# Loading an attention output projection's weights in two whole-tile transfers, split by rows instead of columns

## The chip, the cores and the metric

The kernel runs on one core of one Trainium2 chip. The metric is the device time of one execution in microseconds. Five engines of the core matter here: TensorE (matmuls), VectorE, ScalarE, GpSimd (POOL) and SyncE (SP), which here only issues DMAs. DMAs issued by SP and by POOL are carried out by the core's 16 DMA engines. Before the change, three runs gave 818.97, 821.54 and 822.07 us, a median of 821.54 us.

## The reference

The input `x` is 2048 rows of 1024 (bfloat16). It is normalised by rows (layer norm without weights). From the result `xn` two branches are computed and joined:

- branch A: `qkv = xn @ wqkv` (1024 by 3072), 32 heads of 32 columns each. Each position attends to 8 positions: itself and those 2, 4, ... 14 before it. The softmax-weighted sum of `v` is multiplied by `wo` (1024 by 1024).
- branch B: `h = silu(xn @ w1) * (xn @ w3)` (each 1024 by 3584), then `h @ w2` (3584 by 1024).

```
s = _A_ref(xn, A_wqkv, A_wo)          # ends in  o.reshape(B, S, D) @ wo
g = silu(_B_ref(xn, B_w1, B_w3, B_w2))
return x + s * g
```

## The kernel before

The 2048 rows are done in four chunks `c` of 512 (`CH`). For a chunk, TensorE does in this order:

1. `qkv` (L273): 24 products of 8 matmuls with `xnT`, the normalised, transposed rows. Chunk 0 has these between its first blocks of `w1` and `w3`.
2. `up_block` (L258) for 14 blocks `fb`: two column groups of `w1` and two of `w3`, each product 8 matmuls. ScalarE applies silu, VectorE multiplies, and this gives the 28 `ht` tiles.
3. `down_half` (L447) for the first half `dh = 0` of the output columns: 7 blocks `fb` of 16 matmuls, with four accumulators.
4. `down_half` for `dh = 1`; after its third block (sixth in chunk 0), `wo_proj` (L416) is put in: 8 products of 8 matmuls. In the last chunk `wo_proj` comes between the halves, and the second half runs row tile by row tile (`last_half`, L483).

The attention itself runs beside these on VectorE, in pieces handed out by `Side` according to estimated costs. Its data cross partitions by DMAs from POOL: 16 transfers `L<-E` before the softmax (L333) and 16 transfers `Pr<-pb` after it (L374). The products with `v` (L385) and their sums (L396) then give `oT`, the left operand of `wo_proj`.

All code is scheduled by hand: each engine takes its instructions in the order in which they were written. On SP's queue that order is, late in a chunk: the last `w1` and `w3` tiles (L167, from six buffers, asked for three blocks ahead), the output weights (`load_wo`, called after block `fb == 10`, L198), then for each block of `down_half` one `w2` tile (`load_w2`, L185), with a transposing DMA of the next chunk's rows (L676) beside it in the first four blocks. The `w2` tiles have three buffers: the first three of a chunk are loaded long before; the tile for the fourth block is issued when the matmuls of the first are done. In the last chunk there is nothing to transpose. POOL loads the residual `xres` (L472, 1 MB) once per chunk.

`oT` has on partition `r*32 + h` the element `r*8 + j` of head `h`, for `j` from 0 to 7. So the weights must lie the same way: row `h*32 + r*8 + j` of `wo` belongs on partition `r*32 + h`. In DRAM, 8 consecutive rows of `wo` (`j`) form one contiguous run of 16 KB. `load_wo` takes two blocks of 128 partitions by 4096 elements from a pool of nine that the attention's tiles also use. Block `dh` holds all eight `j` and 512 of the 1024 columns, loaded by four DMAs of 32 partitions, with 8 runs of 1 KB for each partition. `wo_proj` uses block `dh` alone for the four products of a column half.

Of the kernel before, what the change touches and what calls it, by code (L numbers as in the profile page):

```python
# [45 lines left out]
def kernel(  # L46
# [11 lines left out]
    nc = tc.nc  # L58
    P = 128
    S, D, F = 2048, 1024, 3584  # L60
    Dh, W, DIL = 32, 8, 2
    KT = D // P
    CH = 512
# [5 lines left out]
    NJ = 8  # L69
    NR = 4  # L70
# [9 lines left out]
    w1_r = B_w1.rearrange("(kt p) f -> p kt f", p=P)  # L80
    w3_r = B_w3.rearrange("(kt p) f -> p kt f", p=P)
    w2_r = B_w2.rearrange("(ft p) n -> p ft n", p=P)
    wo_r = A_wo.rearrange("(h r j) n -> r h j n", r=NR, j=NJ)
    wqkv_r = A_wqkv.rearrange("(kt kp) c -> kp kt c", kp=P)

    const = ctx.enter_context(tc.tile_pool(name="const", bufs=1))
# [19 lines left out]
    def block(name):  # L106
        return blk.tile([P, 4096], BF16, tag="blk", name=name)
# [6 lines left out]
    for st in range(2, NST):  # L114
# [10 lines left out]
        out=ident[:], in_=ident[:], compare_op=ALU.not_equal, fill=1.0,  # L125
# [5 lines left out]
        out=maskb[:], in_=maskb[:], compare_op=ALU.is_ge, fill=-1.0e9,  # L131
# [60 lines left out]

    def load_wo():
        was = []
        for dh in range(2):
            wa = block("wo").rearrange("p (j n) -> p j n", n=CH)
            for r in range(NR):
                nc.sync.dma_start(out=wa[r * 32:(r + 1) * 32, :, :], in_=wo_r[r, :, :, dh * 512:(dh + 1) * 512])  # L198
            was.append(wa)
        return was  # L200


# [205 lines left out]
    def wo_proj(c, was):  # L408
        side.flush()
        oT = att["oT"]  # L410
        s_sb = block("s_sb").rearrange("p (st d) -> p st d", st=NST)
        for dh in range(2):
            for st in range(NST):
                ps = psum_aux.tile([P, CH], FP32, tag="aux", name="ps_wo")
                for j in range(NJ):
                    nc.tensor.matmul(  # L416
                        ps[:], lhsT=oT[:, j, st * P:(st + 1) * P], rhs=was[dh][:, j, :],
                        start=(j == 0), stop=(j == NJ - 1),
                    )
                nc.scalar.copy(out=s_sb[:, st, dh * 512:(dh + 1) * 512], in_=ps[:])  # L420
                side.step(GRP)
        return s_sb
# [131 lines left out]
    def bring0(st):  # L554
# [16 lines left out]
        out=junk[:], in_=x0[2][:], func=ACTF.Square, bias=nm[:], scale=1.0 / 32.0, accum_out=mv0[2][:, 1:2],  # L571
# [54 lines left out]
    for fb in range(1, LEAD):  # L626
        w1t, w3t = take_w(("1", fb)), take_w(("3", fb))
        for i in range(2):
            pss = []
            for wt in (w1t, w3t):  # L630
                ps = psum_mm.tile([P, CH], FP32, tag="mm", name=f"gu0_{fb}_{len(pss)}")
# [7 lines left out]
    for t in range(3):  # L639
        for j in range(NJ):  # L640
            ps = psum_mm.tile([P, CH], FP32, tag="mm", name="ps_qkv")
# [6 lines left out]
        for half in range(2):  # L648
            nc.sync.dma_start(
                out=wperm[half * 4:(half + 1) * 4, :, t * NJ:(t + 1) * NJ, :].rearrange("kt kp j p -> kp kt (j p)"),  # L650
                in_=pmh[t, half].rearrange("kp kt j p -> kp kt (j p)"),
# [5 lines left out]
    for c in range(NCH):  # L657
        if c > 0:
            qkv(c, xnT)
        was = None  # L660
        for fb in range(LEAD if c == 0 else 0, FB):
            blk_hts = up_block(c, xnT, fb)
            hts = hts + blk_hts if hts is not None else blk_hts
            if fb == 10:
                was = load_wo()
# [14 lines left out]
        if c + 1 < NCH:  # L680
            state = {}

            def mid(fb, c=c):
                if fb == (WO_AT if c else WO_AT0) - 1:
                    state["s"] = wo_proj(c, was)
                    for st in range(NST):
                        side.add(1.38, lambda st=st: finish(c, st, 0, 512, gts[st], state["s"], xres, nc.gpsimd))

            gts1 = down_half(c, 1, hts, mid)
            side.flush()  # L690
            s_sb = state["s"]
            for st in range(NST):
                side.add(1.38, lambda st=st, c=c, gts1=gts1, s_sb=s_sb, xres=xres: finish(
                    c, st, 512, 512, gts1[st], s_sb, xres, nc.gpsimd))
            xnT = xnT_next
            hts = None
        else:
            s_sb = wo_proj(c, was)
            for st in range(NST):
                finish(c, st, 0, 512, gts[st], s_sb, xres, nc.gpsimd)  # L700
            last_half(c, hts, s_sb, xres)
# [30 lines left out]
```

## Time and profile before

| | before |
|---|---|
| median of three runs | 821.54 us |
| profiled execution | 819.93 us |
| its span, first to last instruction | 818.2 us |
| TensorE matmul busy | 808.8 us (99%), 3817 matmuls |
| VectorE, ScalarE, POOL busy | 481.4, 206.1, 95.3 us |
| mean granted TensorE clock | 0.999 |
| DMA: data, mean rate | 152.69 MB, 187 GB/s |
| `wo` loads | 32 issues of 256 KB, median 9.2 us from issue to landing |
| `w1`, `w3`, `w2` loads | 168 issues of 512 KB, median 4.6 us from issue to landing |
| `wo_proj` matmuls (L416) | 256, in the chain with 13.81 us per chunk |

A line of the page's groups gives the line of the code, the engine and operation, the tiles written and read with their sizes, the count, and then busy time and mean duration. Matmul durations overlap, since matmuls are pipelined. "SPq" is an instruction that SP's queue handles without SP being busy, DMA issues among them. In the list of waits, the last three numbers are the total in us, how many times, and the longest. In the chain in order of time, they are the start, the length in us, and the work with its count. In a timeline, the first two numbers are start and length of a merged group of instructions. In a table of windows, the columns are the window, its length, busy time of TensorE, its weight loads, VectorE, ScalarE and POOL with counts, the clock, the DMA share and the rate in GB/s. The DMA share is the busy time of packets over 16 engines; packets that overlap can bring it above 1.

### The profile page before, as it was taken

The page shows a single profiled execution, that of the slowest core. Times are in us where ns is not written, and L with a number is a line of the kernel's source. Part 1 is how long each engine was busy: PE and PEld are TensorE (multiplying, and loading weights), DVE is VectorE, ACT ScalarE, POOL GpSimd, SP SyncE. Part 2 cuts the span into 40 slices and gives each one's busy share as a digit, 9 for nine tenths or more (in the row PEclk, how much of TensorE's full clock was granted, in tenths as well). Part 3 has the DMA queues.
Part 4 walks back from the last instruction along what each step waited for, and adds up shares of the span by engine and source line. Part 5 has one row for each costly group of instructions (what it writes and reads, how often), then busy time and mean ns, then how long its engine had stood idle before and what let it go on. Part 6 is the DMA issues. An engine that isn't in the chain of part 4 may idle for free.

```text
span 818.2 us, 9549 instructions
## 1 busy us (share of the span) xinstructions
PE 808.8 (99%) x3817; PEld 372.5 (46%) x3817; DVE 481.4 (59%) x489; ACT 206.1 (25%) x319; POOL 95.3 (12%) x176
## 2 busy tenths in 40 slices
PE   8999999999999999999999999999999999999997
PEld 5444444444444444444444444444444444444444
DVE  6619947693229765692224968489111695759432
ACT  6552133011432132101133213310223321311120
POOL 0000041301100223000110030400000004130010
PEclk9999999999999999999999999999999999999999
DMA  9992698795454786879255588869925548696810
GB/s 289 347 371 74 195 211 194 167 307 180 130 149 140 219 193 182 180 197 307 87 180 153 144 221 181 196 134 230 295 92 180 152 133 203 167 210 144 255 51 26
DMA packets 221085, 152.69 MB, mean 187 GB/s; under 512 B 19568, under 2 KB 209136, under 8 KB 221040
## 3 DMA queue, kind: packets, MB, share of 16 engines
q1 hardware_dynamic: 214224, 135.55, 60.8%
q0 software_dynamic: 6528, 16.26, 8.1%
q8 instruction: 30, 0.49, 0.2%
q10 hardware_dynamic: 288, 0.26, 0.1%
q14 instruction: 15, 0.12, 0.1%
HBM read 130.02 MB, written 10.49 MB: 172 GB/s over the span
## 4 chain that ended last, share of the span: by engine, by line
PE 97%; DMA 2%; ACT 0%; DVE 0%; SPq 0%; issue 0%
PE gu L258 45%; PE ps_qkv L273 20%; PE acc L447 19%; PE ps_wo L416 7%; PE acc L483 3%; DMA wt<-in_B_w_dram 2%; PE gu L273 2%; PE gu L584 1%; DMA x<-in_A_x_dram 0%; PE tp L543 0%; ACT xnT L547 0%; ACT junk L560 0%; SPq L112 0%; DVE x L207 0%; DVE gt L433 0%
## 5 line engine op out<-in xcount | busy, mean ns | idle before, releaser
L258 PE MATMUL gu<-xnT_next,wt 128*128 128x512 bf16 x1344 | 290.6, 379 | 0.0
L258 PEld LDWEIGHTS <-wt 128*128 128x128 bf16 x1696 | 166.0, 98 | 200.1
L447 PE MATMUL acc<-wt,ht 128*128 128x512 bf16 x784 | 170.7, 379 | 1.3 <-DMA wt<-in_B_w_dram 1.3
L247 DVE TENSOR_TENSOR ht<-sg,gu 128x512 bf16<-128x512 bf16 x112 | 75.8, 680 | 92.1 <-PE gu L258 67.6
L245 ACT ACTIVATE sg<-gu 128x512 bf16<-128x512 f32 x112 | 65.9, 597 | 247.7 <-PE gu L258 232.8
L273 PE MATMUL ps_qkv<-xnT_next,wt 128*128 128x512 bf16 x576 | 124.8, 379 | 0.0
L303 DVE TENSOR_TENSOR prod<-qT,kT 128x4096 bf16<-128x4096 bf16 x32 | 73.1, 2285 | 86.4 <-ACT kT L277 86.3
L447 PEld LDWEIGHTS <-ht 128*128 128x128 bf16 x784 | 76.7, 98 | 94.1 <-issue 1.8
L273 PEld LDWEIGHTS <-wt 128*128 128x128 bf16 x640 | 62.6, 98 | 75.3
L433 DVE TENSOR_TENSOR gt<-gt,s_sb 128x512 f32<-128x512 f32 (+1 forms) x33 | 22.2, 674 | 122.0 <-ACT gt L427 63.3
L258 PE MATMUL gu<-xnT,wt 128*128 128x512 bf16 x352 | 76.1, 379 | 0.0
L333 POOL DMA_DIRECT2D L<-E x64 | 37.1, 587 | 295.0 <-DVE E L318 190.1
L385 DVE TENSOR_TENSOR pv<-Pr,vT 128x4096 bf16<-128x4096 bf16 x28 | 63.2, 2283 | 0.0
L314 DVE TENSOR_TENSOR prod<-prod 128x2048 bf16<-128x2048 bf16 x64 | 61.1, 955 | 1.4
L416 PE MATMUL ps_wo<-wo,oT 128*128 128x512 bf16 x256 | 55.9, 379 | 0.0
L427 ACT ACTIVATE gt<-acc 128x512 f32<-128x512 f32 (+1 forms) x33 | 19.3, 584 | 141.1 <-PE acc L447 119.6
L374 POOL DMA_DIRECT2D Pr<-pb x64 | 36.8, 583 | 107.6 <-DVE pb L367 101.9
L273 PE MATMUL ps_qkv<-xnT,pm 128*128 128x512 bf16 x192 | 41.6, 379 | 0.0
L435 POOL DMA_DIRECT2D out_dram<-o_t x28 | 15.3, 545 | 209.4 <-DVE o_t L434 204.9
L416 PEld LDWEIGHTS <-oT 128*128 128x128 bf16 x256 | 25.0, 98 | 30.2
L420 ACT CAST s_sb<-ps_wo 128x512 bf16<-128x512 f32 x32 | 18.7, 585 | 77.9 <-PE ps_wo L416 77.9
L396 DVE TENSOR_TENSOR oT<-oT,pv 128x4096 bf16<-128x4096 bf16 x16 | 36.6, 2288 | 0.3
(67 smaller groups left out, 371.4 us busy)
## 6 DMA issues: line engine op xcount, KB each, us to landing
wt<-in_B_w_dram SPq DMA_DIRECT2D x168, 512.0 KB, 4.6
wt<-wperm SPq DMA_DIRECT2D x36, 512.0 KB, 5.4
wo<-in_A_wo_dram SPq DMA_DIRECT2D x32, 256.0 KB, 9.2
raw<-in_A_wqkv_dram SPq DMA_DIRECT2D x6, 1024.0 KB, 10.2
wperm<-pm SPq DMA_DIRECT2D x6, 1024.0 KB, 9.4
L<-E POOLq DMA_DIRECT2D x64, 64.0 KB, 5.8
Pr<-pb POOLq DMA_DIRECT2D x64, 64.0 KB, 4.2
xres<-in_A_x_dram POOLq DMA_DIRECT2D x4, 1024.0 KB, 6.9
```

The lines of the kernel that those rows point to most:

```text
L245: nc.scalar.activation(out=sg[:], in_=g_ps[:], func=ACTF.Silu)
L247: nc.vector.tensor_mul(ht[:], sg[:], u_ps[:])
L258: nc.tensor.matmul(ps[:], lhsT=wt[:, kt, i * P:(i + 1) * P], rhs=xnT[:, kt, :], start=(kt == 0), stop=(kt == KT - 1),)
L273: nc.tensor.matmul(ps[:], lhsT=lhs(kt), rhs=xnT[:, kt, :], start=(kt == 0), stop=(kt == KT - 1))
L303: nc.vector.tensor_mul(prod, qT[:], kT[:, :, o:o + CH])
L314: nc.vector.tensor_add(prod[:, 0:n, :], prod[:, 0:n, :], prod[:, n:2 * n, :])
L333: nc.gpsimd.dma_start(out=L4[sq * 32:(sq + 1) * 32, r, :, :], in_=E[r * 32:(r + 1) * 32, :, sq * P:(sq + 1) * P],)
L374: nc.gpsimd.dma_start(out=Pr[r * 32:(r + 1) * 32, :, sq * P:(sq + 1) * P], in_=pb[sq * 32:(sq + 1) * 32, :, :],)
L385: nc.vector.tensor_mul(dst, Pr[:, w, :].unsqueeze(1).to_broadcast([P, NJ, CH]), vT[:, :, o:o + CH])
L396: nc.vector.tensor_add(a, a, b)
L416: nc.tensor.matmul(ps[:], lhsT=oT[:, j, st * P:(st + 1) * P], rhs=was[dh][:, j, :], start=(j == 0), stop=(j == NJ - 1),)
L447: nc.tensor.matmul(accs[st][:], lhsT=hts[f][:, st * P:(st + 1) * P], rhs=w2t[:, i, :], start=(f == 0), stop=(f == FT - 1),)
```

## The change

The view of `wo` in DRAM now has `j` and the columns as one contiguous dimension of 8192 elements. A block holds half of that dimension: four of the eight `j`, with all 1024 columns. It is loaded by one DMA of 1 MB with one run of 8 KB for each of the 128 partitions. In `wo_proj`, each product of 8 matmuls takes its first four from one block and its last four from the other. The issue's place in SP's queue, the blocks' sizes and the matmuls' sizes stay as they are.

```
-    wo_r = A_wo.rearrange("(h r j) n -> r h j n", r=NR, j=NJ)
+    wo_r = A_wo.rearrange("(h r j) n -> r h (j n)", r=NR, j=NJ)
...
     def load_wo():
         was = []
-        for dh in range(2):
-            wa = block("wo").rearrange("p (j n) -> p j n", n=CH)
-            for r in range(NR):
-                nc.sync.dma_start(out=wa[r * 32:(r + 1) * 32, :, :], in_=wo_r[r, :, :, dh * 512:(dh + 1) * 512])
-            was.append(wa)
+        for half in range(2):
+            wa = block("wo")
+            nc.sync.dma_start(out=wa[:], in_=wo_r[:, :, half * 4096:(half + 1) * 4096])
+            was.append(wa.rearrange("p (j n) -> p j n", n=D))
         return was
...
                 for j in range(NJ):
                     nc.tensor.matmul(
-                        ps[:], lhsT=oT[:, j, st * P:(st + 1) * P], rhs=was[dh][:, j, :],
+                        ps[:], lhsT=oT[:, j, st * P:(st + 1) * P], rhs=was[j // 4][:, j % 4, dh * 512:(dh + 1) * 512],
                         start=(j == 0), stop=(j == NJ - 1),
                     )
```

## The prediction

> **What bounds the kernel now.** I read four views in this order: the page's busy rows and chain, the table of waits, the windows around the output-weight loads, and SyncE's timeline with the landings of its DMAs.
>
> The page and the chain come first.
>
> ```profile
> PE 808.8 (99%) x3817; PEld 372.5 (46%) x3817; DVE 481.4 (59%) x489; ACT 206.1 (25%) x319; POOL 95.3 (12%) x176
> PEclk9999999999999999999999999999999999999999
> PE 97%; DMA 2%; ACT 0%; DVE 0%; SPq 0%; issue 0%
> ```
>
> TensorE is the bound: busy for 808.8 of 818.2 us at the full granted clock, and 97% of the chain. The waits say how much a better-timed transfer could give back:
>
> ```profile
> PE acc L447 <- DMA wt<-in_B_w_dram: 1.3, 2, 1.0
> ```
>
> TensorE waits 1.3 us in the whole run for weights, always for the down projection's (L447), never for `wo`. So the change can gain hardly more than 1.3 us, and its reach downward is set by what it does to transfers that TensorE does need. The chain, in order of time, gives the deadlines:
>
> ```profile
> 149.33 10.37 PE acc L447 x48
> ...
> 350.05 34.53 PE acc L447 x160
> ...
> 550.35 6.92 PE acc L447 x32
> ...
> 751.78 24.17 PE acc L447 x112
> ```
>
> The down projection of the four chunks starts at 149.33, 350.05, 550.35 and 751.78 us. Its `w2` tiles have three buffers, filled long before; the fourth tile is asked for when the first has been used. Three tiles take 10.37 us of matmuls (the first of these lines), so that fourth tile must have landed by 159.7, 360.4, 560.7 and 762.1 us.
>
> SyncE's timeline, in chunk 0, has the `wo` loads and what comes next on the queue:
>
> ```profile
> 129.06 6.41 SPq L198 DMA_DIRECT2D wo<-in_A_wo_dram  x8
> 152.81 0.39 SPq L185 DMA_DIRECT2D wt<-in_B_w_dram  x1
> 153.29 1.34 SPq L676 DMA_TRANSPOSE xnT_next<-x_t  x1
> ```
>
> The other chunks issue `wo` from 329.78, 530.08 and 731.82. Between `wo` and that fourth `w2` tile, SyncE issues nothing for 17 us.
>
> Then the windows (us; busy times of five engines; clock; DMA share; GB/s), one with nothing but `wo` on the DMA engines and one of large 128-partition loads at the start:
>
> ```profile
> 137.00:139.50 2.50, 2.50 (x14) 1.12 (x12) 2.43 (x4) 0.60 (x1) 0.00 (x0) 1.00 1.13 219
> 40.00:50.00 10.00, 10.00 (x48) 4.55 (x47) 2.01 (x2) 6.62 (x9) 0.00 (x0) 1.00 1.09 374
> ```
>
> Both keep the 16 DMA engines full (shares of 1.13 and 1.09), yet `wo`, which goes to 32 partitions at a time, gets 219 GB/s, or 13.7 per engine, where the other gets 374, or 23.4 per engine. The landings of the `wo` transfers, and of the weights of the last stage (755 to 776):
>
> ```profile
> DMA to landing us min/median/max: 7.0/9.2/11.1
> DMA to landing us min/median/max: 3.4/3.7/4.8
> ```
>
> **The change, part by part.**
>
> *Fewer issues.* 32 `wo` issues at a median of 478 ns become 8: some 11.5 us less on SyncE's queue. Zero for the end: SyncE is otherwise idle for those 17 us. The last of each chunk's eight issues also waits for an earlier weight tile (135.16 in chunk 0); that goes too, with nothing queued behind it. If that cover were gone, 6 us per chunk would stand ahead of the `w2` issue; it is not.
>
> *Matmuls.* 256 of them (L416), still 128x512 from contiguous runs of 512 columns: no change at 379 ns each. Every product now needs both tiles, and both are held to the end of `wo_proj`, 7 us longer for the first (half of the 13.81 us of L416). Their blocks come up again nine allocations later, in the next chunk's attention, over 40 us on: zero. The later landing of the pair costs nothing while it stays ahead of 194.65, 384.59, 586.02 and 775.96, when `wo_proj` starts.
>
> *The transfer itself.* Same 2.1 MB per chunk, in runs of 8 KB instead of 1 KB. What decides is over how many DMA engines it is spread. Every transfer in this trace has an outermost count of 32 or 128, a multiple of 16. The new source is (r, h, columns) with an outermost count of 4, and it can't be merged: h steps over 32 rows, r over 8. No row shows such a transfer. The bounds are 16 engines, if it is dealt out by the tile's 128 rows, and 4 engines, if by the source's outermost dimension. I take 4, because 4 units can't be dealt out evenly to more, and because the nearest rows (`wo` before, 32 units) leave no remainder that would show another way.
>
> The Trainium skill ("DMA: Bandwidth & Descriptors", section on why a DMA increments its semaphore by 16) has a rule for this which speaks against the change: a transfer uses the largest number of engines up to 16 that divides the slowest counts of both sides, here 4 and 128, hence 4. No row here shows it for a count under 16.
>
> *With 4 engines*, each carries 524 KB per chunk. At 23.4 GB/s that takes 22.4 us, at 13.7 it takes 38.3 us. I take 38.3: the low rate is `wo`'s own row, for writes into one group of 32 partitions, and the four shares walk through four such groups in step, on 4 partitions at a time, which is narrower still. The Trainium skill ("SBUF — State Buffer", "Door 1: The DMA port swizzle") says that partitions p and p+32 share a port, which would pair the shares two by two; the 219 against 374 GB/s agrees with such sharing.
>
> Start of the stream: the old first transfer landed 7.0 us after its issue, 1.2 us of which was its own 256 KB at 219 GB/s; with some 1 us for completion (an estimate: half of the 2.0 us that the fastest 512 KB landing, 3.4 us, has over 1.4 us at 374 GB/s), it began 4.8 us after the issue, behind the weight tiles queued before it. End: 129.06 + 4.8 + 38.3 = 172.2, and 372.9, 573.2, 774.9.
>
> *What stands behind it.* The fourth `w2` tile has its share on all engines, those four too, behind `wo` on the same queue. After `wo` ends it takes 1.4 us of data and 1 us of completion. Landing 174.6 against a need at 159.7: TensorE waits 14.9 us in chunk 0. Chunk 1: 375.3 - 360.4 = 14.9; chunk 2: 575.6 - 560.7 = 14.9; chunk 3: 777.3 - 762.1 = 15.2. Sum 59.9 us.
>
> *POOL's transfers on the same engines.* `xres` (1 MB, four times) and, in chunk 0, the 16 `Pr` transfers (1 MB, issued 139.8 to 150.0) put 65.5 KB each on those engines while they are busy: five times 2.8 us at 23.4 GB/s if it all adds up, five times 4.8 at 13.7, nothing if they fill gaps that the paired engines leave. Bounds 0 and 24 us; I take 7, half of the middle, since an engine that serves POOL leaves its partner alone for that time. Late `Pr` would delay the `oT` products on VectorE, which end at 185.6 against 194.65 in chunk 0: 9 us of cover, and more once TensorE itself is late.
>
> *After the stall*, the next `w2` tiles and, in chunks 0 to 2, the transposes queue on the four engines in the order of need, 49 KB on each per 3.45 us of matmuls, 2.1 us of work at the one rate and 3.6 at the other: 0 to 2 us per chunk, 3 us in all. The old waits of 1.3 us merge into the stalls.
>
> Sum: 59.9 + 7 + 3 - 1.3 = 68.6 us on the profiled execution's 819.9: 888.5. The median of the runs shown is 1.6 us above that execution, so 890.
>
> **The rivals.**
>
> *A. Four engines at the full rate*, or part of the way there, since the shares can drift apart and the long runs may be faster. `wo` then ends at 156.3, 357.0, 557.3, 759.0. The four stalls are about 1.8 us each (chunk 0: 156.3 + 2.4 + 2.8 for `Pr` - 159.7; chunks 1 to 3: 0 to -1 from `wo` and 2.8 from `xres`): 7 - 1.3, and the time is 827. Each 1 us more per chunk adds 4, so 30 us per chunk gives 857. For it: the 374 GB/s. Against it: `wo`'s own row.
>
> *B. All 16 engines* (not slower; also that the change does nothing that can be seen). 2.1 MB at 219 to 374 GB/s take 5.6 to 9.6 us and end about 144, as the old ones did, nearly 9 us before the next `w2` issue. TensorE then waits as before: 820 to 822. It decides from 5 engines at 23.4 GB/s each, or 8 at 13.7: `wo` is then through by 153, when the next `w2` tile is issued. For it: every transfer of this kernel so far is evenly spread. Against it: the outermost count of 4.
>
> *C. The pair is late for `wo_proj` itself.* Under 4 engines `wo` lands by 775.9 in chunk 3, whose `wo_proj` starts at 775.96 before any stall. It can't be the wait that ends last, as the `w2` tile stands behind it on the same engines: 0 us more than the main case. For it only a slower stream than 13.7 would speak; then the time is over 905.
>
> **How the numbers follow.** Main case (4 engines, 33 to 38 us per chunk or a little over): 0.47, with 868 to 910 as its own range (4 x 5 us less, or 17 us more from POOL). A: 0.36, between 824 and 868. B: 0.14, 820 to 822. C, beyond 905: 0.03. A tells from B only above 0.5% (4 us, about what a measurement of this kernel can tell): A gives slower but for its edge. Slower 0.85, same 0.13, faster 0.02, as there are only 1.3 us to win. The range from 824 to 905 leaves out B and the far end.
>
> **What would show it.** Right: `wo` has 8 issues of 1024 KB with landings of 25 and 43 us; a wait of `acc` L447 for DMA `wt` of about 15 us in each chunk, 60 to 70 in all, and the chain with some 8% DMA; DMA share well under half, some 55 GB/s, in the windows from 137 to 150. A would have the same lines with a stream of 90 GB/s and waits under 2 us. B would have landings under 15 us, and the waits unchanged. Wrong also if TensorE waits for something else: `ps_wo` for DMA `wo`, or the L385 products for `Pr`.

## The result, and the profile after

The changed kernel takes 854.43 us (853.57 to 854.8) against 821.81 us for the kernel before on the same chip: a ratio of 1.0398, with a 95% interval of 1.0374 to 1.0423. It is 32.6 us slower, where 68.6 us had been forecast. The profiled execution took 853.57 us, with a span of 851.8 us against 818.2.

The page of the changed kernel, in the lines that answer to those shown of before, with the count of packets of SyncE's queue (`q1`) and the issues of `wo`:

```profile
PE 815.0 (96%) x3743; PEld 375.5 (44%) x3817; DVE 481.5 (57%) x489; ACT 206.2 (24%) x319; POOL 95.4 (11%) x176
PEclk9999999899999999989999999998999999999899
q1 hardware_dynamic: 206576, 135.55, 58.0%
PE 89%; DMA 7%; another core or an unknown queue 3%; issue 1%; ACT 0%; DVE 0%; SPq 0%; DVEq 0%
wo<-in_A_wo_dram SPq DMA_DIRECT2D x8, 1024.0 KB
```

TensorE has fallen from 99% to 96%, and there are now four dips in its clock, one per chunk (the records of 74 matmuls are missing from this trace: the program still has 3817). DMA has risen from 2% to 7% of the chain. The same kernel's list of waits names where:

```profile
PE acc L446 <- DMA wt<-in_B_w_dram: 24.3, 4, 6.9
```

Four waits, one per chunk, 24.3 us in all instead of 1.3. Line 446 is the down projection (447 before). SyncE's timeline and the chain show which tile it was in chunk 0:

```profile
130.66 1.31 SPq L197 DMA_DIRECT2D wo<-in_A_wo_dram  x2
154.41 0.38 SPq L185 DMA_DIRECT2D wt<-in_B_w_dram  x1
154.88 8.49 SPq L675 DMA_TRANSPOSE xnT_next<-x_t  x1
```

```profile
154.41 12.35 DMA wt<-in_B_w_dram
```

The first `w2` tile asked for after `wo` takes 12.35 us to land; before the change, the fastest such tile took 3.4. The windows of the changed kernel (columns as before; the last three are granted clock, DMA share and GB/s) show the stream of `wo`, and then the matmuls just after the wait:

```profile
344.00:350.00 6.00, 6.00 (x30) 2.70 (x29) 5.24 (x4) 1.19 (x2) 0.00 (x0) 1.00 0.25 68
350.00:362.00 12.00, 11.95 (x56) 5.49 (x56) 12.00 (x8) 1.79 (x3) 0.00 (x0) 1.00 0.26 104
...
166.80:172.30 5.50, 5.50 (x14) 1.97 (x14) 5.33 (x3) 0.00 (x0) 0.00 (x0) 0.51 1.10 300
```

While `wo` is alone on the DMA engines, a quarter of them is busy: 4 of 16. In this chunk they move 68 GB/s at first and 104 later. After the wait TensorE runs for 5.5 us at a granted clock of 0.51: 14 matmuls where some 25 would fit.

The count of packets settles the number of engines. SyncE's queue before the change:

```profile
q1 hardware_dynamic: 214224, 135.55, 60.8%
```

Now there are 206,576 packets, 7,648 fewer. The data of `wo` account for 7,168 (8.4 MB in 1024 packets of 8 KB instead of 8192 of 1 KB). The other 480 are packets of 4 bytes. In these traces every transfer ends with one such packet on each engine that it uses (ScalarE's queue, with 2 transfers on 16 engines, has 32 of them). The 32 transfers of `wo` on 16 engines made 512, and the missing 480 leave 32, that is 4 for each of 8 transfers.

The balance, from the starts of the matmuls: waits of 5.7, 5.7, 6.6 and 7.1 us, 25.0 in all and 23.4 more than before. After them 13, 12, 9 and 7 matmuls start 427 ns apart instead of 216, which costs 8.3 us. The first `qkv` matmul comes 1.6 us later. The sum is 33.3 of the 33.6 us that the span has grown. The 1.6 us aren't from the change: that start lies between 31.3 and 34.9 us in the traces below, whatever the kernel does with `wo`.

### The profile page after: what moved, and what is told of

It reads as the page before. It is cut to its first block, busy times and chain, and to the rows that moved or that the text cites. A ratio compares the mean times of both kernels' runs of the same rounds, so it can differ in the third digit from the quotient of the medians.

```text
span 851.8 us, 9432 instructions
## 1 busy us (share of the span) xinstructions
PE 815.0 (96%) x3743; PEld 375.5 (44%) x3817; DVE 481.5 (57%) x489; ACT 206.2 (24%) x319; POOL 95.4 (11%) x176
## 3 DMA queue, kind: packets, MB, share of 16 engines
q1 hardware_dynamic: 206576, 135.55, 58.0%
## 4 chain that ended last, share of the span: by engine, by line
PE 89%; DMA 7%; another core or an unknown queue 3%; issue 1%; ACT 0%; DVE 0%; SPq 0%; DVEq 0%
PE gu L257 40%; PE ps_qkv L272 19%; PE acc L446 17%; PE ps_wo L415 6%; DMA wt<-in_B_w_dram 6%; PE acc L482 3%; PE gu L272 2%; PE gu L583 1%; DMA x<-in_A_x_dram 0%; PE tp L542 0%; ACT xnT L546 0%; ACT junk L559 0%; SPq L197 0%; SPq L112 0%
## 5 line engine op out<-in xcount | busy, mean ns | idle before, releaser
L446 PE MATMUL acc<-wt,ht 128*128 128x512 bf16 x768 | 178.4, 392 | 25.1 <-DMA wt<-in_B_w_dram 24.3
L446 PEld LDWEIGHTS <-ht 128*128 128x128 bf16 x784 | 78.7, 100 | 123.9 <-issue 36.8
```

What stands on the lines that cost most here:

```text
L446: nc.tensor.matmul(accs[st][:], lhsT=hts[f][:, st * P:(st + 1) * P], rhs=w2t[:, i, :], start=(f == 0), stop=(f == FT - 1),)
```

## The experiments

The theory: the source's leading count of 4 puts each transfer on 4 engines, and the next `w2` tile stands behind it there. The rivals: the long runs or the few large transfers block what follows; or it is the blocks by rows, of which every product needs both.

### Four groups of 32 partitions, 8 KB runs kept

```
-            nc.sync.dma_start(out=wa[:], in_=wo_r[:, :, half * 4096:(half + 1) * 4096])
+            for r in range(NR):
+                nc.sync.dma_start(out=wa[r * 32:(r + 1) * 32, :], in_=wo_r[r, :, half * 4096:(half + 1) * 4096])
```

> Each half is loaded by four transfers of 32 partitions instead of one of 128; the runs of 8 KB and the blocks by rows stay. Theory (the leading count of 4 puts a transfer on 4 DMA engines, and the next w2 tile waits behind it on them): a leading count of 32 brings back 16 engines; 2.1 MB per chunk at some 219 GB/s, done 9 us before the next w2 tile is asked for; no wait of L446 beyond the old 1.3 us, full clock, 819 to 823 us. Rival 1 (the long runs or the few large transfers block the weights behind them): still a wait of 4 to 7 us per chunk, 845 to 856. Rival 2 (both blocks are needed by every product and are held longer): the loss stays whole, 854.

Measured: 820.69 us, ratio 1.0011 (0.998 to 1.0041). `q1` has 207,056 packets: 480 more than the changed kernel, hence 16 engines again. No wait of the down projection for weights is left in the list. Its window with `wo`:

```profile
337.00:344.00 7.00, 6.95 (x33) 3.16 (x33) 5.77 (x4) 1.18 (x2) 0.00 (x0) 1.00 1.02 222
```

Long runs, blocks by rows and products that need both blocks are all still there, and the loss is gone, so none of these is its cause. The transfers here are small again; few large ones are tried two kernels further on. At 222 GB/s against 219 before, the run's length did nothing for the rate of a 32-partition transfer either.

### Blocks by columns, 1 KB runs, all 128 partitions

```
-            for r in range(NR):
-                nc.sync.dma_start(out=wa[r * 32:(r + 1) * 32, :, :], in_=wo_r[r, :, :, dh * 512:(dh + 1) * 512])
+            for j in range(NJ):
+                nc.sync.dma_start(out=wa[:, j, :], in_=wo_r[:, :, j, dh * 512:(dh + 1) * 512])
```

(an edit of the kernel before)

> The blocks by columns and the 1 KB runs of the kernel before, but each of the 16 transfers per chunk covers all 128 partitions with a leading count of 4. Theory: 4 engines again; a share of 0.25 of the DMA engines in the windows with wo alone; 524 KB per engine in 512 runs, 24 to 42 us; stalls of 1 to 17 us per chunk, 835 to 900 us. Rival 1 (long runs): no long runs, 819 to 823. Rival 2 (both blocks needed by every product): this kernel needs one block per product as before, 819 to 823.

Measured: 828.99 us (825.01 to 832.94), ratio 1.0106 (1.0065 to 1.0147): slower than before, if less than the theory's lower end. Its count of packets, 213,968, is what 64 transfers with 4 closing packets each give (206,576 - 1,024 - 32 + 8,192 + 256). The waits and a window:

```profile
PE acc L447 <- DMA wt<-in_B_w_dram: 11.5, 5, 7.0
```

```profile
350.00:357.00 7.00, 6.95 (x33) 3.19 (x33) 7.00 (x7) 0.60 (x1) 0.59 (x1) 1.00 0.27 96
```

So a leading count of 4 costs time without any long run, on 4 engines (a share of 0.27). The stalls are half as long as with 8 KB runs; why the shorter runs fare better was not tried.

### Rows in plain order

```
-    wo_r = A_wo.rearrange("(h r j) n -> r h (j n)", r=NR, j=NJ)
+    wo_r = A_wo.rearrange("(p j) n -> p (j n)", j=NJ)
...
-            nc.sync.dma_start(out=wa[:], in_=wo_r[:, :, half * 4096:(half + 1) * 4096])
+            nc.sync.dma_start(out=wa[:], in_=wo_r[:, half * 4096:(half + 1) * 4096])
```

> As the changed kernel, two transfers of 1 MB in 8 KB runs to 128 partitions, but partition p gets rows 8p to 8p+7, so that the source has one dimension of 128 runs. The rows of wo are in another order than the attention output's, so the output is not the reference's; all work is done. Theory: 16 engines, and all ports at once: 340 to 380 GB/s while wo is alone on the engines, against 219 before; no new wait, 819 to 823 us. Rival 1 (few large transfers, long runs): 845 to 856.

Measured: 820.97 us, ratio 1.0002 (0.9986 to 1.0019), 96 closing packets more than the changed kernel (8 x 16 instead of 8 x 4). Its window:

```profile
334.00:339.00 5.00, 5.00 (x25) 2.29 (x24) 4.56 (x3) 1.19 (x2) 0.00 (x0) 1.00 0.97 397
```

The same two transfers of 1 MB in 8 KB runs, with one dimension of 128 rows in place of 4 times 32, run on all engines at 397 GB/s and cost nothing: few large transfers aren't the cause either. They gain nothing either: `wo` was never waited for.

### Two groups per transfer

```
+            for r in (0, 2):
+                nc.sync.dma_start(out=wa[r * 32:(r + 2) * 32, :], in_=wo_r[r:r + 2, :, half * 4096:(half + 1) * 4096])
```

> Each half is loaded by two transfers of 64 partitions with a leading count of 2. Theory: 2 engines, a share of 0.13 of the DMA engines while wo is alone, at 27 GB/s where the two write the same port and 50 where not. The changed kernel's streams took 25.7 to 32.3 us on 4 engines; twice that, some 60, adds about 30 us to every chunk's stall: 854 + 120 = 974, between 920 and 1040. Rival (the size of the transfers or of the runs matters, not the number of engines): transfers of half the size, 835 to 854.

Measured: 927.9 us, ratio 1.1314 (1.1264 to 1.1365). 16 transfers leave the same 32 closing packets as 8 did, hence 2 engines.

```profile
PE acc L447 <- DMA wt<-in_B_w_dram: 95.8, 4, 26.0
```

```profile
133.00:139.00 6.00, 5.95 (x29) 2.70 (x28) 4.23 (x4) 2.75 (x4) 0.00 (x0) 1.00 0.13 39
...
160.00:172.00 12.00, 0.00 (x0) 0.00 (x0) 11.93 (x6) 0.00 (x0) 0.77 (x1) 0.61 0.12 52
```

Half the engines, about four times the wait. The streams lasted 47 to 52 us, not the 60 expected, since two engines reach 52 GB/s once under way.

### Which engines hinder each other

Both kernels load two of the four groups alone (16 engines) and the other two in one transfer on 2 engines, after them. Of the first:

```
+            for r, k in ((0, 1), (3, 1), (1, 2)):      # second kernel: ((2, 1), (3, 1), (0, 2))
+                src = wo_r[r:r + k] if k > 1 else wo_r[r]
...
+                nc.sync.dma_start(out=wa[r * 32:(r + k) * 32, :], in_=src)
```

> Each half in three transfers: groups 0 and 3 with a leading count of 32, then groups 1 and 2 (partitions 32 to 95) in one transfer with a leading count of 2. Theory (two engines slow each other only where they write partitions p and p+32 at the same time; partitions 32 to 63 and 64 to 95 never do): the two engines run at 50 to 53 GB/s together from the start, some 20 us for both halves; no stall, 819 to 823 us. Rival (few engines are slow for another reason, such as the reads): starts at 37 GB/s as in the kernel with two groups.

> As the other three-transfer kernel, but the pair is groups 0 and 1 (partitions 0 to 63), after groups 2 and 3. Theory: the two engines start in step on partitions p and p+32: 27 to 40 GB/s at first, rising as they drift apart; 22 to 28 us for both halves; 819 to 826 us. Rival: the same rate over time as the pair of groups 1 and 2.

Measured, one time each: 849.16 and 869.15 us. The windows at the start of the pair's stream, partitions 32 to 95 first, then partitions 0 to 63:

```profile
344.00:350.00 6.00, 6.00 (x29) 2.74 (x28) 6.00 (x4) 0.99 (x2) 0.00 (x0) 1.00 0.14 55
```

```profile
354.00:360.00 6.00, 6.00 (x29) 2.71 (x28) 6.00 (x6) 1.19 (x2) 0.00 (x0) 1.00 0.14 34
361.00:367.00 6.00, 6.00 (x30) 2.70 (x28) 6.00 (x5) 0.60 (x1) 0.77 (x1) 1.00 0.14 46
```

The rates are as the theory has them: 55 GB/s at once for partitions 32 to 95, and 34 rising to 46 for partitions 0 to 63. The expectations' words "p and p+32" are too wide, though: partitions 32 to 63 and 64 to 95 lie 32 apart as well and did not hinder each other, so it holds only inside one half, as for 0 to 31 with 32 to 63. The times are not as expected. The stream of all of `wo` lasts 27 to 32 us in one kernel and 34 to 37 us in the other, beyond its cover, the time until the `w2` tile behind it is needed. The likely reason, worked out and not tried, is that the same two engines carry their share of the other two groups and of POOL's transfers too, which both expectations left out. The 20 us between the two kernels, from one execution of each, fit that hindrance.

### The same transfers in pieces, earlier

```
-            if fb == 10:
-                was = load_wo()
+            if fb in (7, 8, 10):
+                load_wo(fb, was)
```

(after block 7 two of the eight `j`, after block 8 two, after block 10 the other four)

> Still transfers with a leading count of 4, but spread: half of the first block's rows after block 7 of up_block, the other half after block 8, the second block after block 10 as before. Theory (the loss is the length of the stream less the 25 us of cover): the stream after block 10 is half as long, 13 to 16 us, and ends before the next w2 tile is asked for; the earlier pieces of 7 to 8 us stay inside the three blocks of lead that the w1 and w3 tiles have; no stall, 819 to 826 us. Rival (four-engine transfers cost something wherever they stand): 840 or more.

Measured: 829.79 us, ratio 1.0109 (1.0087 to 1.0131). The list of waits:

```profile
PEld L258 <- DMA wt<-in_B_w_dram: 8.4, 6, 3.9
PE gu L258 <- DMA wt<-in_B_w_dram: 6.2, 3, 3.4
PE acc L447 <- DMA wt<-in_B_w_dram: 1.8, 2, 1.3
```

The down projection's waits are gone but for 1.8 us, so the changed kernel's loss was the length of the stream beyond its cover. It misses the expected 819 to 826 because the weights of blocks 11 to 13, which now stand behind the pieces, come up to 3.9 us late.

### From ScalarE's queue

```
-            nc.sync.dma_start(out=wa[:], ...)
+            nc.scalar.dma_start(out=wa[:], ...)
```

> The changed kernel with the two transfers issued from ScalarE's queue instead of SyncE's. If what counts is that the w2 tile stands behind wo in order on the same queue, its own queue now lets it through: landing 4 to 8 us after its issue as before, stalls of 0 to 2 us, 820 to 832 us. If what counts is the four engines, which are full in either case, and the two queues take turns there by packets, the w2 tile lands when wo is nearly through: 848 to 857.

Measured: 894.33 us, ratio 1.0885 (1.0853 to 1.0916): worse than either answer.

```profile
PE gu L257 <- DMA wt<-in_B_w_dram: 54.8, 3, 20.8
PE acc L446 <- DMA wt<-in_B_w_dram: 11.6, 3, 10.6
```

The tiles of `w1` and `w3` show why, in the view of their line from 335 to 350 us (four issues, with the landings of two):

```profile
DMA to landing us min/median/max: 13.1/22.7/32.3
```

They were issued between 335.5 and 344.2 us, `wo` from its own queue at 342.5. On SyncE's queue all of them stand ahead of `wo`, and in the changed kernel the last ones landed within 6.4 us. Here `wo` no longer waits for them but shares four of their engines at once, and a tile of 512-byte packets, issued 1.7 us after `wo`, took 32.3 us to land beside packets of 8 KB. In chunk 0 the `w2` tile landed 0.9 us after the last packet of `wo`, although it came from another queue. So for the tile behind `wo` the engines are what counts, not the order in the queue, and that order even protects what stands ahead.

### Keeping TensorE busy

```
             w2t = take_w2((c, dh, fb))
+            if dh == 0 and fb == 3:
+                idle = psum_aux.tile([P, CH], FP32, tag="aux", name="idle_ps")
+                for _ in range(25):
+                    nc.tensor.matmul(idle[:], lhsT=warm[:, 0:P], rhs=warm[:], start=True, stop=True)
```

> The changed kernel with 25 matmuls on a tile of zeros ahead of the down projection's fourth block in each chunk; their results are not used. They take 5.4 us at the full clock, inside the waits of 5.5 to 7 us for the w2 tile. Theory (an idle TensorE is granted half the clock and gets it back only after some matmuls): the 8 to 13 matmuls at 427 ns after each stall run at 216 ns; 2 us less per chunk, 844 to 848 us, and a clock of 0.99 or more. Rival (the slow matmuls come from the weights landing late or from DMA traffic, not from idling): slow as before, 853 to 856.

Measured: 852.08 us, spread over 847.5 to 857.84; ratio to the kernel before 1.0381 (1.0329 to 1.0434), an interval that takes in the changed kernel's own 1.0398. Part of its timeline:

```profile
162.62 5.56 PE L444 MATMUL idle_ps<-warm 128*128 128x512 bf16 x25
168.01 17.43 PE L450 MATMUL acc<-wt,ht 128*128 128x512 bf16 x78
...
592.76 0.59 PE L450 MATMUL acc<-wt,ht 128*128 128x512 bf16 x1 [4.63 <-DMA wt<-in_B_w_dram]
```

In three chunks no slow matmuls follow, as here: 78 matmuls from 168.01 on at the full rate. In chunk 2 a later tile was 4.63 us late, and the half clock came back. The clock behaved as the theory says, but the time did not show the gain: waits and added matmuls together made 33.9 us here against 25.0. So the question went to a kernel without late DMAs.

### Idling without a late DMA

The kernel with four groups, with TensorE held up by ScalarE (N = 4 or 10):

```
+            if dh == 0 and fb == 3:
+                idle = psum_aux.tile([P, CH], FP32, tag="aux", name="idle_ps")
+                nc.tensor.matmul(idle[:], lhsT=warm[:, 0:P], rhs=warm[:], start=True, stop=True)
+                for _ in range(N):
+                    nc.scalar.copy(out=warm[:], in_=idle[:])
+                nc.tensor.matmul(idle[:], lhsT=warm[:, 0:P], rhs=warm[:], start=True, stop=True)
```

> The kernel with four groups of 32 partitions and 8 KB runs (no stall), in which TensorE is made to idle once per chunk before the down projection's fourth block: one matmul on zeros, 4 copies of its result by ScalarE of some 0.6 us each, and one matmul that needs the copy. Gap 2.4 us and some 0.5 us of hand-over. Theory (TensorE keeps its clock over short waits and loses it over those above 4 to 5 us, as the waits of up to 3.6 us and from 5 us on in the runs so far suggest): no slow matmuls, 4 x 3 = 12 us over that kernel, 831 to 835. Rival (any wait costs clock, or none does): the short and the long gap differ only by their lengths.

> As the kernel with the short gap, but 10 copies: 6 us and the hand-over, about as long as the stalls of the changed kernel. Theory: 4 x 6.6 of idling, and after each gap 8 to 13 matmuls at 427 ns instead of 216, 2.3 us more, with no DMA late: 855 to 859, granted clock about 0.98. Rival (the slow matmuls belong to the late DMA): 4 x 6.6 alone, 845 to 849, clock 0.99 or more.

The kernel with the long gap first gave a median of 853.61 us, but its profiled execution took 1712.73 us. The trace below is of the same kernel, run again:

> The kernel with the long gap once more, for its trace: the short gap's trace showed 7 or 8 matmuls at half clock after three of its four gaps of 2.7 us, though no DMA was late there. If idling alone takes the clock, each of the four gaps of 6.8 us is followed by 7 to 14 slow matmuls, 1.4 to 2.9 us each, and the time is 853 to 860. If the slow matmuls come only with late weights, none follow, and the time is 848 to 850.

Measured: 837.64 us with the short gap (ratio 1.0182, 1.014 to 1.0223), 854.91 us with the long one (1.0409, 1.0338 to 1.0481). The long gap's timeline, then its windows in the gap and after it:

```profile
159.10 0.38 PE L444 MATMUL idle_ps<-warm 128*128 128x512 bf16 x1
165.71 0.61 PE L447 MATMUL idle_ps<-warm 128*128 128x512 bf16 x1 [6.23 <-ACT warm L446]
```

```profile
159.30:165.70 6.40, 0.18 (x1) 0.00 (x0) 6.33 (x4) 5.85 (x10) 0.00 (x0) 0.91 1.10 294
165.70:171.30 5.60, 5.59 (x14) 2.01 (x15) 5.57 (x4) 0.00 (x0) 0.00 (x0) 0.50 0.11 24
```

And after two of the four short gaps:

```profile
164.60:167.00 2.40, 2.40 (x12) 1.10 (x13) 2.37 (x2) 0.00 (x0) 0.00 (x0) 1.00 0.77 262
368.00:371.40 3.40, 3.39 (x9) 1.19 (x10) 3.37 (x3) 0.00 (x0) 0.00 (x0) 0.50 0.59 141
```

Idling alone takes the clock. After the four gaps of 6.4 us 13, 9, 7 and 6 matmuls are slow, 7.6 us in all. The sum 820.7 + 4 x 6.4 + 1.7 for the added matmuls + 7.6 gives 855.6, and 854.9 was measured. The short gap refutes the limit of 4 to 5 us: after gaps of 2.7 us the clock was kept once and lost three times, 4.7 us in all. Here the same sum gives 837.9, and 837.6 was measured.

## Why the prediction was right or wrong

*The bound, and nothing to gain: right.* With 16 engines and either layout the time is that of before (ratios 1.0011 and 1.0002), whatever the issues on SyncE, the length of the runs and the need for both blocks.

*Four engines: right*, by the share, by the packets, and by the longer stalls with 2 engines. The Trainium skill's rule in "DMA: Bandwidth & Descriptors" (section on why a DMA increments its semaphore by 16: the largest divisor of both leading counts, up to 16) agrees with the counts tried: 4 engines for 4, 2 for 2, 16 for 32 and 128.

*The place of the stall: right.* In each chunk it is the `w2` tile asked for first after `wo`. The stream began at 133.7 us in chunk 0 against 133.9 worked out, which is partly luck: in this run the down projection starts 1.4 us later than before, at 150.8. What counts for the stall is the time from the stream's start to the need for the tile, taken as 25.8 us (25.5 in chunk 3). It was 27.5, 26.4, 26.3 and 27.5 us, which makes the stalls 4.7 us shorter in all.

*The rate of the stream: wrong, and this is the step that failed.* "I take 38.3" rested on 13.7 GB/s per engine for the whole way, "in step". From the first to the last 8 KB packet the streams took 31.3, 25.7, 29.7 and 32.3 us, 29.8 on average, with POOL's share in it, for which 1.75 us per chunk had come on top of 38.3. That is 10 us too much in each chunk. That the engines hinder each other in pairs was right, as far as the two pair kernels show it: the pair on partitions 0 to 63 begins at 34 GB/s where the pair on 32 to 95 has 55. What failed is its duration. The four engines begin at 64 to 74 GB/s, 16 to 18 each, and then become faster: in chunk 1 they move 104 GB/s from 350 to 362 us, 26 each, which is above the 23.4 taken as the upper rate, and in chunk 2 88 GB/s from 560 to 570 us. That they fall out of step is the likely reading; no trace shows the single engines. The 32-partition transfers on 16 engines show no such rise (219 GB/s before, 222 with four groups), and so that row was not a measure of the new transfer's later part.

*The clock after the stall: left out.* The sum took a stall at its own length. Each one costs 1.4 to 2.7 us more at half clock, 8.3 us in all: a quarter of the loss.

*The tail: sized too low; what queues after it: too high.* 2.4 us was taken from the end of `wo` to the landing of the tile; it was 1.8, 6.3, 3.1 and 2.1 us, 3.7 us more in all, with 6.3 where `xres` was issued within 0.1 us of it. The 3 us for later tiles did not come: there is one wait per chunk.

*The terms together.* For the waits, 59.9 + 7 = 66.9 us had been forecast. Less 41.1 for the streams and 4.7 for their starts, plus 3.7 for the tails, that is 24.8; 25.0 was measured.

*Rival A* named the right middle: 30 us per chunk gave 857. That it lies so near 854.4 is partly luck, since it counted POOL's share on top of the stream and had no half clock. *Rival B* is what the kernels with 16 engines show, *rival C* never showed: no wait of `ps_wo` for `wo`.

## What to carry to other kernels

Before two dimensions of a DRAM view are merged into one transfer, look at the count that ends up outermost. Here counts of 4 and 2 put the transfer on 4 and 2 DMA engines, counts of 32 and 128 on all 16, and every later transfer on that queue waits behind it on these few engines. With 8 KB runs, four transfers with a leading count of 32 or one with 128 were both better than one with 4. A stall of TensorE as long as these is to be priced with the half clock that follows it.

## What the runs showed of the hardware that was not expected

- TensorE can lose its clock in a gap as short as 2.7 us, in three of four gaps of the same length; it came back after 6 to 13 matmuls of 512 columns. A wait of 3.6 us in the kernel with the pieces cost no clock. The clock records of these traces tell the cases apart. In each trace but the one of 1712.73 us, the clock changes only on a grid of 3.41 us. After the first 20 us it fell to half at the end of every full-clock slot of that grid in which TensorE idled for 2.24 us or more (29 slots), and of none in which it idled for 2.15 us or less. The short gaps that lost the clock put 2.69, 2.39 and 2.24 us into one slot; the one that kept it was split into 1.32 and 1.38 us, and the wait of 3.6 us into 2.12 and 1.43. The Trainium skill ("TensorE: Matmul & The Clock Gate", "What's actually happening") tells of half the clock after an idle window of some 3.4 us that runs freely. The free-running grid fits. That the whole window has to be idle doesn't fit the 2.24 us, and the measurement decides.
- A second queue gave no way around busy engines: 512 KB in small packets took up to 32.3 us to land beside a stream of 8 KB packets on 4 engines.
- Two engines writing partitions 0 to 31 and 32 to 63 begin at 34 GB/s together instead of 55, but become faster by themselves, to 46 some 7 us later; in the kernel with two groups a pair reaches 52. What frees them was not tried.
